# Three of eight top-k masks taken from VectorE and given to ScalarE and GpSimd

## The chip, the cores and the metric

One core of a Trainium2 chip runs the whole program. The metric is device time in microseconds (us) of one execution, median of several runs. TensorE (PE), VectorE (DVE), ScalarE (ACT), GpSimd (POOL) and SyncE (SP, which issues most DMAs) each take their instructions in program order and wait for one another through semaphores.

## The reference

Three stages follow one another: attention in which every query keeps only its 32 largest scores, a routed layer with one expert for each token, and a layer of four experts that are all used.

```python
# attention: batch 2, 8 heads, 576 tokens, head width 64
scores = scale * np.matmul(q, k.transpose(0, 1, 3, 2))
kth = np.partition(scores, -top_k, axis=-1)[..., -top_k:-top_k + 1]     # top_k = 32
scores = np.where(scores >= kth, scores, -1e9)
attn = np.exp(scores - scores.max(-1, keepdims=True))
attn = attn / (attn.sum(-1, keepdims=True) + 1e-9)
x = np.matmul(attn, v)                                    # then 1152 rows of 512
# first layer: 8 experts, 512 -> 1024 -> 512, each token goes to the argmax of its logits
out[mask] = gate_w[mask, None] * (np.maximum(x[mask] @ w1[e], 0) @ w2[e])
# second layer: 4 experts, all of them, weighted by the normalised domain_probs
out += p[:, e:e + 1] * (np.maximum(x @ w1[e], 0) @ w2[e])
```

## The kernel before

The 1152 tokens are nine tiles of 128 rows, in three groups: tiles 0 and 1, tiles 2 to 4, tiles 5 to 8. Attention makes x tile by tile; the two expert layers work on a whole group. While the layers of one group run, attention of the next group's tiles is mixed in; the first group's attention has nothing to be mixed with, and the last group's layers have no attention beside them.

Attention goes by units: a unit is one tile and one pair of heads, `hp` (0 to 3), with `i` = 0 or 1 for the head in the pair. Its steps are laid out by hand: `at_step(n, fn, ...)` puts a call at step `n` of a plan (in half steps), a unit starts every 8 steps (`b0 = SP * j`), and `attention` is a generator that emits one half step at a time. During the expert layers, `pace` advances it in proportion to the TensorE work emitted. So program order on each engine is fixed when the program is built.

For one head the steps are: `sc_mm` (scores, TensorE), `sc_ev` (copy to SBUF, ACT, L465), `top_max` and `top_rep` in turn, four and three times (MAX8 at L477, MATCH_REPLACE8 at L486, DVE), which leave the 32 largest scores in `m`; `p_exp` (exp of the scores, ACT, L494) into a buffer `e0` or `e1` of which there is one each; `p_mask` (L499, DVE), which multiplies `e` by (score >= 32nd score); `p_hi` (half-precision part and row sum, ACT, L514); `p_lo` (the remainder, POOL, L523); `p_tr` (transposing DMA, SP, L528) into `pt`; and `pv_mm` (product with v, TensorE, L553), seven steps after `p_hi`. `finish_tile` (L577) divides by the row sum and gives the rows `xrow`.

In the expert layers every weight block is split in two parts, `whi` (ACT, L1010) and `wlo` = weight - `whi` (L1018, most of them on POOL, some on DVE). TensorE forms `hps` (L1134), ACT and DVE split its ReLU into `hhi` (L1148) and `hlo` (L1151), and TensorE forms `y` (L1107), which ACT or DVE add up in `acc` (L1186, L1188). Transposes `xtp` (L1036) bring rows to the layers. Around the start of a group, small DVE operations choose experts (`gate`, `pick`, `assign`, `compact`; TensorE's `ips` at L916 reads their result `pg` of L906), and POOL fetches rows with gathers (`yg`, L1226).

Of the kernel before, what the change touches and what calls it, by code (L numbers as in the profile page):

```python
# [14 lines left out]
ACTF = mybir.ActivationFunctionType  # L15
ALU = mybir.AluOpType
# [3 lines left out]
TOPK = 32  # L20
# [24 lines left out]
PV0 = 17  # L45
# [4 lines left out]
def kernel(  # L50
# [15 lines left out]
    nc = tc.nc  # L66
    B, H, S, D = q.shape
# [7 lines left out]
    scale = 1.0 / float(D) ** 0.5  # L75
# [27 lines left out]
    with tc.manual_schedule():  # L103
# [116 lines left out]
        def attention(at, start):  # L220
# [58 lines left out]
            units = [(t, hp) for g in GROUPS for t in g for hp in range(H // 2)]  # L279
            NP = len(units)  # L280
            st = {}
# [5 lines left out]
            def at_step(n, fn, *args, half=0):  # L287
                plan.setdefault(round(2 * n) + half, []).append((fn, args))
# [200 lines left out]
            def p_exp(j):  # L489
                z = st[j]  # L490
                z["e"] = []
                for i in range(2):
                    e = w_p.tile([128, S], F32, tag=f"e{i}", name="e")
                    nc.scalar.activation(out=e, in_=z["s", i], func=ACTF.Exp, bias=z["nb"][:, i:i + 1], scale=scale)  # L494
                    z["e"].append(e)

            def p_mask(j, i):
                z = st[j]
                nc.vector.scalar_tensor_tensor(  # L499
                    out=z["e"][i], in0=z["s", i], scalar=z["m"][:, i, TOPK - 1:TOPK], in1=z["e"][i],  # L500
                    op0=ALU.is_ge, op1=ALU.mult)
# [149 lines left out]
            for j in range(NP):  # L651
                b0 = SP * j
                t, hp = units[j]
                lag = PV_LAST[GROUP_OF[t]] if hp == H // 2 - 1 and t in LAST else PV_LAG
                if j:

                    late = t == MIX or (t == MIX + 1 and hp == 0)
                    b2 = -4 if j == 1 else b0 - 9 if late else b0 - 16
                    at_step(b2, q_tr, j)
                    at_step(b2 + 1, q_ev, j)  # L660
                    for i in range(2):
                        at_step(b0 - 5 + 2 * i, sc_mm, j, i)
                        at_step(b0 - 4 + 2 * i, sc_ev, j, i)
                at_step(b0 + 1, top_nb, j)
                at_step(b0 + 5, p_exp, j)
                for i in range(2):
                    b1 = b0 - 1 if (j, i) == (0, 0) else b0
                    for r in range(4):
                        at_step(-18 if (j, r, i) == (0, 0, 0) else b1 + 2 * r, top_max, j, r, i, half=i)
                        if r < 3:  # L670
                            at_step(b1 + 2 * r + 1, top_rep, j, r, i, half=i)
                    at_step(b1 + 7, p_mask, j, i, half=i)
                for i in range(2):
                    at_step(b0 + 8 + i, p_hi, j, i)
                    at_step(b0 + 9 + i, p_lo, j, i)
                    at_step(b0 + 10 + i, p_tr, j, i)
                    at_step(b0 + (lag if j else PV0) + i, pv_mm, j, i)
                if hp == H // 2 - 1:
                    for n in range(3):
                        at_step(b0 + lag - 2 + n, row_factor, t, n)  # L680
                    at_step(b0 + lag + 2, finish_tile, t)
                if hp == 0 and j:
                    at_step(b0 - 28, ld, "q", q, t)
                    b3 = b0 - 16 if t == MIX + 1 else b0 - 21
                    at_step(b3, q_hi, t)
                    at_step(b3 + 1, q_lo, t, nc.gpsimd)
                    at_step(b3 + 3, q_two, t)
# [576 lines left out]
        at = ctx.enter_context(ExitStack())  # L1264
        start = ctx.enter_context(ExitStack())
        att = attention(at, start)
        done = set()

# [214 lines left out]
```

## Time and profile before

| what | us |
|---|---|
| median of 3 runs (918.04 to 923.94) | 921.47 |
| the profiled execution, its own time | 922.85 |
| span of that execution, first to last instruction | 921.1 |
| PE busy in the span | 815.3 |
| DVE busy | 659.2 |
| POOL busy | 534.6 |
| ACT busy | 496.6 |

Rows of the trace speak of the profiled execution, whose time is 1.75 us above its span and 1.38 us above the median. Busy times of PE count pipelined matmuls, so a busy PE is not PE at its peak. Time positions below are microseconds from the start of the span.

### The profile page before, as it was taken

What the parts mean: (1) busy time and instruction counts of PE and PEld (TensorE: products, weight loads), DVE (VectorE), ACT (ScalarE), POOL (GpSimd) and SP (SyncE); (2) the same over time, 40 slices, a digit from 0 to 9 for tenths busy, and PEclk for the clock granted to TensorE, in tenths of its full rate; (3) what the DMA queues carried; (4) which work ended last, traced back from release to release, by engine and by line L of the source; (5) the groups of instructions that cost most, each with busy time, mean ns of one, the idle gap of its engine ahead of it and who ended that gap; (6) DMA issues with size and microseconds to landing.
All of it is one profiled execution on the core that took longest, in us unless ns stands there. A gap on an engine that the chain in (4) does not pass through costs nothing. (4 is left out here: it accounts for less than half of the span.)

```text
span 921.1 us, 15133 instructions
## 1 busy us (share of the span) xinstructions
PE 815.3 (89%) x5277; PEld 696.2 (76%) x5277; DVE 659.2 (72%) x1309; ACT 496.6 (54%) x1017; POOL 534.6 (58%) x469
## 2 busy tenths in 40 slices
PE   5555576999999987999979999998999899999995
PEld 4444365887888876888859888877888688888884
DVE  5999969998989989999989899944434431123212
ACT  6857644765768654677637664633355242432220
POOL 3664456986787975778738676755346343333320
PEclk7675577999999998999989999999999999999998
DMA  7464534867675754679666464554456433322201
GB/s 133 82 128 84 139 104 118 220 177 182 166 184 121 193 157 137 201 180 257 170 122 177 126 172 131 134 148 135 148 163 228 139 115 97 109 91 92 92 23 50
DMA packets 197627, 129.60 MB, mean 141 GB/s; under 512 B 129122, under 2 KB 172130, under 8 KB 197540
## 3 DMA queue, kind: packets, MB, share of 16 engines
q1 hardware_dynamic: 196500, 125.12, 51.2%
q0 software_dynamic: 1040, 3.41, 1.3%
q8 instruction: 43, 0.70, 0.3%
q14 instruction: 44, 0.36, 0.1%
HBM read 98.62 MB, written 6.30 MB: 114 GB/s over the span
## 5 line engine op out<-in xcount | busy, mean ns | idle before, releaser
L1018 POOL TENSOR_TENSOR wlo<-wraw,whi 128x512 fp32r<-128x512 f32 x278 | 364.4, 1332 | 251.1 <-ACT whi L1010 212.6
L1151 DVE SCALAR_TENSOR_TENSOR hlo<-hps,hhi 128x256 fp32r<-128x256 f32 (+3 forms) x168 | 83.7, 498 | 189.0 <-ACT hhi L1148 188.6
L1010 ACT ACTIVATE whi<-wraw 128x512 fp32r<-128x512 f32 x336 | 193.5, 624 | 26.0 <-DMA wraw<-in_moe_w_dram 25.9
L1148 ACT ACTIVATE hhi<-hps 128x256 fp32r<-128x256 f32 (+3 forms) x168 | 75.2, 448 | 230.0 <-PE hps L1134 221.2
L1107 PE MATMUL y<-whi,hhi 128*128 128x512 f32 x440 | 177.6, 404 | 1.0 <-ACT acc L1186 0.6
L1107 PE MATMUL y<-wlo,hhi 128*128 128x512 f32 x440 | 173.4, 394 | 1.1 <-POOL wlo L1018 1.1
L1107 PE MATMUL y<-whi,hlo 128*128 128x512 f32 x440 | 172.9, 393 | 0.6 <-DVE hlo L1151 0.6
L1134 PE MATMUL hps<-x,whi 128*128 128x256 f32 (+2 forms) x768 | 169.3, 344 | 4.2 <-DVE hlo L1151 2.6
L477 DVE MAX8 m<-w 128x8 f32<-128x576 f32 x216 | 154.0, 742 | 0.0
L1134 PEld LDWEIGHTS hps<-x,whi 128*128 128x128 f32 x768 | 131.1, 192 | 19.1 <-DVE hlo L1151 3.7
L523 POOL TENSOR_TENSOR pbuf<-e,pbuf 128x576 f16<-128x576 f32 (+1 forms) x80 | 109.5, 1368 | 48.9 <-ACT pbuf L514 45.3
L486 DVE MATCH_REPLACE8 w<-m,w 128x576 f32<-128x576 f32 x144 | 105.9, 739 | 0.0
L1107 PEld LDWEIGHTS y<-whi,hlo 128*128 128x128 f32 x440 | 83.0, 189 | 19.2 <-DVE hlo L1151 0.9
L1107 PEld LDWEIGHTS y<-whi,hhi 128*128 128x128 f32 x440 | 83.9, 191 | 14.0 <-ACT acc L1186 1.0
L1107 PEld LDWEIGHTS y<-wlo,hhi 128*128 128x128 f32 x440 | 83.8, 190 | 13.3 <-POOL wlo L1018 1.7
L1134 PE MATMUL hps<-x,wlo 128*128 128x256 f32 (+2 forms) x384 | 86.0, 343 | 0.0
L273 PE MATMUL sps<-kst,qs 128*128 128x288 f32 x320 | 64.8, 333 | 19.5 <-ACT s_sb L465 9.5
L499 DVE SCALAR_TENSOR_TENSOR e<-s_sb,m,e 128x576 f32<-128x576 f32 x72 | 78.3, 1115 | 1.1 <-ACT e L494 1.0
L553 PEld LDWEIGHTS <-pt 128*128 128x128 f16 (+3 forms) x1200 | 48.8, 106 | 36.0 <-DMA pt<-pbuf 16.3
L514 ACT ACTIVATE pbuf<-e 128x576 f16<-128x576 f32 (+1 forms) x80 | 54.2, 678 | 38.4 <-DVE e L499 38.0
L553 PE MATMUL pv<-vst,pt 128*128 128x64 f16 (+3 forms) x1200 | 61.8, 203 | 14.8 <-DMA pt<-pbuf 12.8
L273 PEld LDWEIGHTS sps<-kst,qs 128*128 128x128 f32 x320 | 52.9, 212 | 27.7 <-ACT s_sb L465 12.9
(181 smaller groups left out, 1074.2 us busy)
## 6 DMA issues: line engine op xcount, KB each, us to landing
wraw<-in_moe_w_dram SPq DMA_DIRECT2D x168, 512.0 KB, 3.9
x_scr<-xrow SPq DMA_DIRECT2D x9, 256.0 KB, 2.1
out_dram<-acc SPq DMA_DIRECT2D x9, 256.0 KB, 2.3
kraw<-in_k_dram SPq DMA_DIRECT2D x16, 128.0 KB, 3.0
vraw<-in_v_dram SPq DMA_DIRECT2D x8, 256.0 KB, 4.2
qraw<-in_q_dram SPq DMA_DIRECT2D x7, 256.0 KB, 4.6
y_scr<-yr SPq DMA_DIRECT2D x6, 256.0 KB, 4.0
pt<-pbuf SPq DMA_TRANSPOSE x72, 4.6
```

Of the source, the lines that this page charges most:

```text
L273: nc.tensor.matmul(out=ps[:, f, 0:HALF], lhsT=qq[:, n, :], rhs=kst[:, h, b * S + f * HALF:b * S + (f + 1) * HALF], start=(j == 0), stop=(j ...
L477: nc.vector.max(out=z["m"][:, i, 8 * r:8 * r + 8], in_=z["s", i] if r == 0 else z["w"][i])
L486: nc.vector.match_replace(out=z["w"][i], in_to_replace=z["m"][:, i, 8 * r:8 * r + 8], in_values=z["s", i] if r == 0 else z["w"][i], imm_va ...
L499: nc.vector.scalar_tensor_tensor(out=z["e"][i], in0=z["s", i], scalar=z["m"][:, i, TOPK - 1:TOPK], in1=z["e"][i], op0=ALU.is_ge, op1=ALU.mult)
L523: nc.gpsimd.tensor_tensor(out=pb[r, 1, o:o + S], in0=z["e"][i][r], in1=pb[r, 0, o:o + S], op=ALU.subtract)
L553: nc.tensor.matmul(out=po[r, h, :], lhsT=l, rhs=rr, start=(n == 0), stop=(n == len(mms) - 1))
L1010: nc.scalar.activation(out=hi, in_=src, func=ACTF.Copy)
L1018: eng.tensor_tensor(out=lo, in0=src, in1=hi.bitcast(F32), op=ALU.subtract)
L1107: nc.tensor.matmul(out=ys[i][0:rows, :], lhsT=l[:, cs], rhs=r[:, 0, :], start=(f == f0 and m == 0), stop=(f == f1 - 1 and m == 2))
L1134: nc.tensor.matmul(out=hp[:, 0:n], lhsT=l[:, c, :], rhs=r[:, c, x0:x0 + n], start=(m == 0), stop=(m == 3 * KD - 1))
L1148: nc.scalar.activation(out=hhi, in_=hp[:, 0:n], func=ACTF.Relu)
L1151: nc.vector.scalar_tensor_tensor(out=hlo, in0=hp[:, 0:n], scalar=0.0, in1=hhi.bitcast(F32), op0=ALU.max, op1=ALU.subtract)
```

## The change

For every tile but the first, and for the second head (`i` = 1) of the first three pairs, that is heads 1, 3 and 5, the DVE instruction of `p_mask` goes. In its place ACT overwrites the score tile twice: relu(kth - score), then exp(-2^126 times that), which is 1 where the score is kept and 0 elsewhere. POOL then multiplies `e` by it. `p_less` (ACT) stands where the mask stood in the plan, the product half a step to one step later, and for these heads `p_hi`, `p_lo`, `p_tr` and `pv_mm` stand two steps later than before. There are 8 x 3 = 24 such heads of 72.

```diff
+            def by_two(j, i):
+                t, hp = units[j]
+                return i == 1 and t > 0 and hp < H // 2 - 1
+
+            def p_less(j, i):
+                z = st[j]
+                s = z["s", i]
+                nc.scalar.activation(out=s, in_=s, func=ACTF.Relu, scale=-1.0, bias=z["m"][:, i, TOPK - 1:TOPK])
+                nc.scalar.activation(out=s, in_=s, func=ACTF.Exp, scale=-(2.0 ** 126))
+
             def p_mask(j, i):
                 z = st[j]
+                if by_two(j, i):
+                    nc.gpsimd.tensor_tensor(out=z["e"][i], in0=z["e"][i], in1=z["s", i], op=ALU.mult)
+                    return
                 nc.vector.scalar_tensor_tensor(
...
-                    at_step(b1 + 7, p_mask, j, i, half=i)
+                    if by_two(j, i):
+                        at_step(b1 + 7, p_less, j, i, half=i)
+                        at_step(b1 + 8, p_mask, j, i, half=i)
+                    else:
+                        at_step(b1 + 7, p_mask, j, i, half=i)
                 for i in range(2):
-                    at_step(b0 + 8 + i, p_hi, j, i)
-                    at_step(b0 + 9 + i, p_lo, j, i)
-                    at_step(b0 + 10 + i, p_tr, j, i)
-                    at_step(b0 + (lag if j else PV0) + i, pv_mm, j, i)
+                    b4 = b0 + i + (2 if by_two(j, i) else 0)
+                    at_step(b4 + 8, p_hi, j, i)
+                    at_step(b4 + 9, p_lo, j, i)
+                    at_step(b4 + 10, p_tr, j, i)
+                    at_step(b4 + (lag if j else PV0), pv_mm, j, i)
```

## Rows read from the trace of the kernel before

**Rows 1.** The page's slices: busy tenths of PE and DVE in 40 slices.
```profile
PE   5555576999999987999979999998999899999995
DVE  5999969998989989999989899944434431123212
```

**Rows 2.** Windows by stage: busy of each engine (instructions), PEclk, DMA, GB/s.
```profile
core 0: us, PE busy (x) PEld busy (x) DVE busy (x) ACT busy (x) POOL busy (x), PEclk, DMA share, GB/s
55.00:121.00 66.00, 36.97 (x291) 28.93 (x289) 64.82 (x154) 42.72 (x86) 27.45 (x32) 0.60 0.54 121
121.00:160.00 39.00, 27.98 (x178) 24.18 (x179) 31.08 (x67) 21.01 (x46) 25.92 (x23) 0.78 0.43 119
160.00:292.00 132.00, 126.31 (x1010) 110.61 (x1009) 124.34 (x247) 93.35 (x203) 104.95 (x84) 1.00 0.70 176
292.00:336.00 44.00, 40.14 (x387) 34.89 (x386) 42.11 (x82) 29.61 (x61) 42.67 (x34) 1.00 0.69 176
336.00:480.00 144.00, 129.41 (x915) 111.90 (x913) 134.04 (x261) 85.40 (x179) 94.89 (x80) 0.94 0.67 175
480.00:604.00 124.00, 124.00 (x859) 108.63 (x858) 118.89 (x228) 76.84 (x155) 86.57 (x74) 1.00 0.58 153
...
640.00:921.00 281.00, 268.24 (x1288) 224.80 (x1286) 82.19 (x125) 97.67 (x184) 104.46 (x81) 0.99 0.36 115
```

**Rows 3.** The same windows, masks of L499 alone: DVE busy (instructions).
```profile
55.00:121.00 66.00, 8.79 (x11) 0.60 0.54 121
...
160.00:292.00 132.00, 19.04 (x16) 1.00 0.70 176
292.00:336.00 44.00, 4.47 (x4) 1.00 0.69 176
336.00:480.00 144.00, 16.95 (x16) 0.94 0.67 175
```

**Rows 4.** Groups by line and form: busy us, mean ns, idle before and its releaser.
```profile
L523 POOL TENSOR_TENSOR pbuf<-e,pbuf 128x576 f16<-128x576 f32 x64 | 87.9, 1373 | 46.1 <-ACT pbuf L514 43.1 <-PE hps L1134 2.2 <-POOL nb L482 0.7
...
L499 DVE SCALAR_TENSOR_TENSOR e<-s_sb,m,e 128x576 f32<-128x576 f32 x72 | 78.3, 1115 | 1.1 <-ACT e L494 1.0
...
L494 ACT ACTIVATE e<-s_sb,nb 128x576 f32<-128x576 f32 x72 | 51.8, 767 | 1.2 <-POOL pbuf L523 1.2
```

**Rows 5.** Lines L499 and L477: ns min/median/max; who waited for L499.
```profile
L499 DVE SCALAR_TENSOR_TENSOR e<-s_sb,m,e x72: 789/808/1912, 21.6 to 602.0; 128x576 f32<-128x576 f32 x72
...
  ACT pbuf L514: 38.0, 22
...
L477 DVE MAX8 m<-w x216: 700/744/755, 12.4 to 600.2; 128x8 f32<-128x576 f32 x108
```

**Rows 6.** Timeline around 343 us, DVE and POOL: start, us, instruction.
```profile
342.28 1.84 DVE L499 SCALAR_TENSOR_TENSOR e<-s_sb,m,e 128x576 f32<-128x576 f32 x1
...
343.47 1.81 POOL L523 TENSOR_TENSOR pbuf<-e,pbuf 128x576 f16<-128x576 f32 x1
```

**Rows 7.** Timeline of DVE at the end of tile 1: start, us, [idle before].
```profile
120.25 0.67 DVE L577 TENSOR_TENSOR xrow<-pv,rd 128x512 f32<-128x512 f32 x1
...
127.19 0.42 DVE L1151 SCALAR_TENSOR_TENSOR hlo<-hps,hhi 128x256 fp32r<-128x256 f32 x1 [3.74 <-ACT hhi L1148]
```

**Rows 8.** What PE waited for, 160 to 604 us: total, times, longest.
```profile
PE ips L916 <- DVE pg L906: 5.3, 1, 5.3
PE xtp L1036 <- DVE acc L1188: 5.1, 2, 3.5
PE pv L553 <- DMA pt<-pbuf: 4.2, 3, 2.7
...
PE y L1107 <- POOL wlo L1018: 1.1, 1, 1.1
```

**Rows 9.** Timeline of POOL around 320 us: start, us, instruction, count.
```profile
312.46 10.29 POOL L1018 TENSOR_TENSOR wlo<-wraw,whi 128x512 fp32r<-128x512 f32 x7
322.70 2.65 POOL L523 TENSOR_TENSOR pbuf<-e,pbuf 64x576 f16<-64x576 f32 x2
```

**Rows 10.** The chain that ended last, one piece: start, us, what.
```profile
461.68 7.90 DMA yg<-y_scr,pos
```

## The prediction, as it was put on record

> **What bounds the kernel now.** I read the slices first, then the windows by stage, then who waits for whom. The slices [rows 1] show two regimes. DVE is at nine tenths almost without a break to about 600 us and then drops to three or four; PE is at five to seven tenths at the start and at nine from about 160 us on. The windows [rows 2] make stages of it. From 55 to 121 us (attention of tile 1, nothing mixed in) DVE is busy 64.82 of 66.00 us while PE has 36.97 and POOL 27.45: DVE alone is the bound. From 160 to 480 us PE and DVE are both nearly full: PE is idle 132.00 - 126.31 = 5.7 us, then 3.9 us (to 336), then 14.6 us (to 480), DVE 7.7, 1.9 and 10.0 us. From 480 to 604 PE shows no idle time at all although DVE is busy 118.89 of 124, so DVE relief buys nothing there. From 640 us on there is no attention and DVE has 82.19 of 281.00 us. So time can be won only from 55 to 121 us, and from the 24.2 us of PE idle time between 160 and 480 us.
>
> What PE waited for in that middle part [rows 8] says who could give it back: 5.3 us for DVE's routing result `pg`, 5.1 us for DVE's `acc`, 4.2 us for transposed probabilities `pt`, which pass ACT, POOL and SP, and only 1.1 us for POOL's `wlo`.
>
> **What the change removes.** 24 masks. At their mean of 1115 ns [rows 4] that is 26.8 us of DVE, at the median of 808 ns [rows 5] 19.4 us. By stage, from the masks that lie there [rows 3]: three of the eleven from 55 to 121 us (heads 1, 3, 5 of tile 1), 8.79 x 3/11 = 2.4 us; six of sixteen from 160 to 292, 7.1 us; one of four to 336, 1.1 us; six of sixteen to 480, 6.4 us. The rest lies where DVE is not late or PE is full.
>
> **What it adds.** On ACT two instructions for each head. The trace has no in-place Relu or Exp of this size, the nearest row is the exp of the same 128x576 tile, 767 ns [rows 4], so 1.53 us a head, 36.8 us in all. ACT has the room: 93.35 of 132.00 us from 160 to 292, the fullest part. Relu (L1148) and Exp (L494) alternate already, so I price no change of function. On POOL a product of two fp32 tiles for each head; nearest is `p_lo` over the same 576 columns, 1373 ns [rows 4], 33 us in all. POOL has 27.1 us free from 160 to 292 and 49.1 from 336 to 480, but 1.3 us from 292 to 336 [rows 2].
>
> **Waits that it adds.** `p_less` waits on ACT for the last MAX8. Behind it in ACT's queue stand `whi`, `hhi` and `sc_ev`. ACT was held at nearly the same place before: 22 of the `p_hi` waited for a mask, 38.0 us in all [rows 5]. The new wait ends one or two masks earlier and is followed by 1.53 us of work, so ACT comes out at most 0.7 us later than after one 0.81 us mask; I take nothing, covered by ACT's idle time. The product waits on POOL for ACT, with `wlo` and the first head's `p_lo` behind it; PE lost 1.1 us to `wlo` in 444 us [rows 8], so a product's 1.4 us is mostly hidden by blocks prepared ahead. `p_hi` of the second head now waits on ACT for POOL, two steps later than it waited for DVE. `p_lo` of that head comes two steps later while the next unit's exp into the same single `e1` stays where it was: 1.2 us of such waits before [rows 4] may become some ten; what covers them is again ACT's idle time. SP gets the second `pt` two steps later, and PE reads it two steps later, so those transposes keep their lead; the first head's `pt` does not move in the plan, though its `p_lo` now stands behind a product on POOL.
>
> **The sum, stage by stage.** *Tile 1, 55 to 121 us:* DVE runs on to `xrow` at 120.25 [rows 7], which starts the first group; three masks less bring it 2.4 us forward. POOL and ACT have the room, so I take all of it: -2.4 (bounds -3.3 at the mean and 0). *121 to 160 us:* DVE waits 3.74 us before its next `hlo` [rows 7], so the mask that goes there gains nothing; `p_less` of tile 2's head 1 falls among the first `whi` and `hhi` and can push the routing by between 0 and 1.5 us: +0.5. *160 to 292:* 7.1 us off DVE against 5.7 us of PE idle time, which is scattered and in part chained (PE, ACT and DVE in turn for transposes): -1.0 (bounds -5.7 and +2). *292 to 336:* here POOL is the late one. Seven `wlo` run for 10.29 us right up to the two `p_lo` at 322.70 [rows 9], and PE's longest wait for `pt` (2.7 us) follows from it. One product goes into this queue: +1.3 (bounds -1.1 if the mask counts instead, +2.7 if two products do). *336 to 480:* the wait of 5.3 us for `pg` ends a DVE run in which one mask took 1.84 us because POOL worked beside it [rows 6]; that mask goes, -1.8. Smaller waits of `hps` for DVE: -1.0. The other large gap is a gather of 7.90 us [rows 10] that POOL starts and the `acc` of rows 8 wait for; a product before it would delay it by 1.4 us, while the `p_lo` that moves two steps later may leave its place in front of it, so 0. Together -2.8 (bounds -6.4 and +1.4). *480 us on:* 0. Sum: -2.4 + 0.5 - 1.0 + 1.3 - 2.8 = -4.4. The profiled execution took 922.85, so 918.4; it lies 1.38 above the median of 921.47, so a median near 917. With the inner bounds of each term the case spans 913 to 922.
>
> **A rule against it.** The rows show first that DVE and POOL disturb one another: a mask beside a POOL operation took 1.84 us [rows 6], one alone 0.81, while MAX8 never leaves 700 to 755 ns [rows 5]. The Trainium skill, Perfetto Trace Analysis, Optimizing Scalar/DVE Operations, warns that since both share an SBUF read port, "offloading operations between those two might not help". The trace agrees for two-input operations and not for MAX8. By the rows the sum keeps its 2.4 and 2.8; by that rule both would be near 0. It is the second rival below.
>
> **The rivals.** *All DVE lag is PE idle time.* If every microsecond of DVE relief from 160 to 480 us came back as PE time, the terms are -2.4, -5.7 (no more idle there), -1.1 and -6.4: 921.5 - 15.6 = 906. For it: DVE has a queue behind it nearly always [rows 2]. Against: the waits named in rows 8 that a mask can shorten are about half of that idle time. *The relief is eaten by contention.* Each product meets one two-input DVE operation and stretches it by 1.84 - 0.81 = 1.03 us: 24.7 us are back on DVE, only the costs of 0.5 and 1.3 stay: 923. Against: after the last MAX8 of a unit DVE does the other mask at once, then mostly MAX8 and MATCH_REPLACE8, and the product starts 1.5 us after. *POOL becomes the bound, slower.* Place: 160 to 336 us, where POOL is busy 147.6 of 176 us and seven products add 9.6 us. If each pushes `wlo` and the first head's `p_lo`, and so `pt`, past what PE has in hand, it costs 9.6 there, 1.4 at the gather and 1.5 in the routing, against the 2.4 won: 921.5 + 10.1 = 932. It decides from the point where POOL's queue is later than the lead of `pt`, as it already is at 322 us; elsewhere POOL still has pauses.
>
> **How the numbers follow.** A measurement of this kernel tells about 1% from no change. The forecast has 0.50 (917, 913 to 922), full relief 0.20 (906), contention 0.18 (923), POOL-bound 0.12 (932). The range for 8 in 10 runs from 905, which takes in most of the full relief, to 929, short of most of the POOL-bound case. Faster by over 1% (below 912.3) is the full relief and a little of the forecast, 0.22; slower by over 1% (above 930.7) is most of the last, 0.11; within, 0.67.
>
> **What would show it.** In the profile after: `xrow` of tile 1 near 117.9 instead of 120.25; DVE busy some 20 to 27 us less, POOL some 33 more, ACT some 37 more; the wait of `ips` for `pg` near 3.5 us; the wait of `pv` around 330 us longer, not shorter; 480 to 604 us as full as before. The prediction is wrong if PE waits for `wlo` or `pt` by more than some 5 us more (POOL), if the 48 masks that stay have a higher mean than 1115 ns (contention), or if PE's idle time from 160 to 480 falls by ten or more.

## The result, and the profile after

The changed kernel takes 934.1 us (median of 4 runs, 931.38 to 935.99), the kernel before 922.64 beside it (918.04 to 923.94): ratio 1.0103, interval 1.007 to 1.0136 (the two medians alone give 1.0124, so the loss is 9.5 to 11.5 us). The forecast was 917.0 with 905 to 929, so the time came out on the other side and outside the range. The profiled execution of the kernel after took 934.64, its span 932.8.

The page's busy times of the kernel after; those of before are in the table ahead of the prediction:

```profile
PE 825.6 (89%) x5277; PEld 704.8 (76%) x5277; DVE 648.4 (70%) x1285; ACT 526.4 (56%) x1065; POOL 562.9 (60%) x493
```

ACT has 29.8 us more and POOL 28.3 more, somewhat less than the forecast 37 and 33. DVE has 10.8 us less, not 20 to 27, and PE has 10.3 us more with the same 5277 matmuls: its work itself became slower.

To see where the time went I matched the k-th `hps` matmul of one trace with the k-th of the other. The kernel after stands +0.1 us against before at 163 us, +3.4 at 298, +7.6 at 311, +4.5 at 366, +11.7 at 378, and from there 11 to 12 to the end. So the loss lies between 163 and 391 us of before, with its largest steps at 298 to 311 and 366 to 378; a third, 3.1 us in small pieces, lies between 231 and 261 us, and 3.2 us are won back between 331 and 351. From 391 us on nothing more is lost. The stretch from 163 to 485 us of before is 163 to 496.5 us after, with the same 2330 matmuls. Windows of the two kernels (columns as in rows 2), before:

```profile
163.00:485.00 322.00, 297.87 (x2330) 259.38 (x2329) 302.42 (x593) 210.31 (x449) 242.32 (x199) 0.97 0.69 176
```

and after, the whole stretch, then the part of it that is 366 to 391 us in before:

```profile
163.00:496.50 333.50, 305.30 (x2330) 265.01 (x2329) 297.77 (x582) 226.81 (x476) 260.26 (x214) 0.95 0.65 171
...
370.50:402.20 31.70, 27.91 (x156) 23.57 (x156) 26.38 (x44) 17.98 (x36) 19.86 (x17) 0.81 0.57 168
```

PE's idle time went from 24.13 to 28.20 us, 4.1 more; the other 7.4 us are PE busy longer over equally many matmuls, at a mean granted clock of 0.95 instead of 0.97. As an estimate from these clocks, (1 - 0.95) x 333.5 - (1 - 0.97) x 322 = 7.0 us, so the clock accounts for nearly all of it. The short stretch took 25.00 us before, at a clock of 0.92, and has 0.81 now.

The new instructions and their neighbours in the kernel after, by form (mean ns of one | idle before and its releaser):

```profile
L515 DVE SCALAR_TENSOR_TENSOR e<-s_sb,m,e 128x576 f32<-128x576 f32 x48 | 56.5, 1194 | 1.9 <-ACT e L494 1.8
L494 ACT ACTIVATE e<-s_sb,nb 128x576 f32<-128x576 f32 x72 | 52.4, 768 | 14.9 <-POOL pbuf L539 14.9
L513 POOL TENSOR_TENSOR e<-e,s_sb 128x576 f32<-128x576 f32 x24 | 35.7, 1486 | 28.3 <-ACT s_sb L508 28.2
L507 ACT ACTIVATE s_sb<-s_sb,m 128x576 f32<-128x576 f32 x24 | 18.6, 773 | 17.0 <-DVE m L477 16.8
L508 ACT ACTIVATE s_sb<-s_sb 128x576 f32<-128x576 f32 x24 | 16.5, 686 | 0.8
```

The sizes are nearly as priced: 773 + 686 = 1459 ns on ACT for a head (forecast 1.53 us) and 1486 ns on POOL (1373). ACT's wait of `exp` for `p_lo` rose from 1.2 us [rows 4] to 14.9.

Who waited for whom in the matched stretch after (us in total, times, longest); rows 8 answer to the PE rows:

```profile
DVE hlo L1172 <- ACT hhi L1169: 16.5, 15, 2.5
ACT s_sb L507 <- DVE m L477: 15.4, 7, 8.4
ACT e L494 <- POOL pbuf L539: 13.6, 6, 3.2
POOL e L513 <- ACT s_sb L508: 7.5, 5, 3.0
PE ips L937 <- DVE pg L927: 6.2, 1, 6.2
PE pv L569 <- DMA pt<-pbuf: 3.5, 3, 1.8
PE qtp L323 <- ACT qs L331: 2.8, 1, 2.8
PE hps L1155 <- DVE hlo L1172: 2.8, 6, 0.7
PE y L1128 <- DVE wlo L1039: 2.1, 1, 2.1
```

PE waits no longer for `pt` than before (3.5 against 4.2) and not for POOL's `wlo`. What grew stands behind ACT: DVE's `hlo` waits 16.5 us for ACT's `hhi` (before, in its matched stretch, 2.5), and PE waits for `hlo` and for ACT's `qs`. An earlier DVE waits longer of itself, so this wait is read again below, beside the relief alone.

The first large step, timeline of the kernel after (start, us, instruction, [idle before]):

```profile
299.69 2.65 POOL L539 TENSOR_TENSOR pbuf<-e,pbuf 64x576 f16<-64x576 f32 x2
...
302.38 0.78 ACT L494 ACTIVATE e<-s_sb,nb 128x576 f32<-128x576 f32 x1 [1.98 <-POOL pbuf L539]
...
305.02 0.78 ACT L507 ACTIVATE s_sb<-s_sb,m 128x576 f32<-128x576 f32 x1
305.83 0.69 ACT L508 ACTIVATE s_sb<-s_sb 128x576 f32<-128x576 f32 x1
...
309.05 0.60 ACT L331 ACTIVATE qs<-qtp 128x512 fp32r<-128x512 f32 x1
...
309.70 0.66 PE L323 MATMUL qtp<-ident,qrow 128*128 128x128 f32 x4 [2.84 <-ACT qs L331]
310.96 0.63 PE L1128 MATMUL y<-whi,hhi 128*128 128x512 f32 x1
```

`p_lo` of the head two steps later holds `e1`, ACT's exp waits 1.98 us for it, `p_less` adds 1.47 us, `qs` is late and PE waits 2.84 us. PE had been busy 2.86 of the 5.50 us from 304 to 309.5, at the full clock. Then the clock falls: this `y` takes 0.63 us where the same form took 0.40 at 303 us, and in the window from 312 to 314 us the granted clock is 0.50, the lower level of 1.2 GHz, with PE busy 2.00 of 2.00 us.

The second large step:

```profile
370.63 0.78 ACT L507 ACTIVATE s_sb<-s_sb,m 128x576 f32<-128x576 f32 x1 [8.37 <-DVE m L477]
...
372.81 1.19 POOL L948 DMA_INDIRECT xg<-x_scr,ixi  x1 [8.47 <-ACT pbuf L530]
...
373.40 5.27 DVE L1039 TENSOR_TENSOR wlo<-wraw,whi 128x512 fp32r<-128x512 f32 x1 [0.22 <-issue]
...
374.04 1.42 POOL L513 TENSOR_TENSOR e<-e,s_sb 128x576 f32<-128x576 f32 x1
375.41 1.28 POOL L539 TENSOR_TENSOR pbuf<-e,pbuf 128x576 f16<-128x576 f32 x1
376.66 0.23 POOL L482 TENSOR_SCALAR nb<-m 128x2 f32<-128x2 f32 x1
376.86 1.26 POOL L1039 TENSOR_TENSOR wlo<-wraw,whi 128x512 fp32r<-128x512 f32 x1
...
378.72 0.51 PE L1128 MATMUL y<-wlo,hhi 128*128 128x512 f32 x1 [2.13 <-DVE wlo L1039]
```

This is head 3 of tile 5. DVE's `wlo`, an operation on two tiles that takes 0.67 us alone, whose `whi` ACT makes behind `p_less`, lasts 5.27 us: it begins beside the gather, POOL then runs the product, `p_lo`, `nb` and its own `wlo` without a pause until 378.12, and DVE is done 0.55 us after that. In before the same DVE instruction met the gather alone:

```profile
369.32 0.67 DVE L1018 TENSOR_TENSOR wlo<-wraw,whi 128x512 fp32r<-128x512 f32 x1
```

### The profile page after: what moved, and what is told of

It is laid out like the page before. It is cut to its first block, busy times and chain, and to the rows that moved or that the text cites. A ratio compares the mean times of both kernels' runs of the same rounds, so it can differ in the third digit from the quotient of the medians.

```text
span 932.8 us, 15107 instructions
## 1 busy us (share of the span) xinstructions
PE 825.6 (89%) x5277; PEld 704.8 (76%) x5277; DVE 648.4 (70%) x1285; ACT 526.4 (56%) x1065; POOL 562.9 (60%) x493
## 4 chain that ended last, share of the span: by engine, by line
PE 61%; DVE 16%; ACT 7%; DMA 6%; issue 4%; POOL 4%; SPq 1%; POOLq 0%; ACTq 0%; DVEq 0%
PE hps L1155 26%; PE y L1128 25%; DVE m L477 4%; DVE w L486 4%; PE pv L569 3%; DMA pt<-pbuf 3%; PE sps L273 3%; POOL wlo L1039 2%; ACT whi L1031 1%; DMA wraw<-in_moe_w_dram 1%; PE xtp L1057 1%; DVE wlo L1039 1%; ACT pbuf L530 1%; DVE hlo L1172 1%; PE qtp L323 1%
## 5 line engine op out<-in xcount | busy, mean ns | idle before, releaser
L477 DVE MAX8 m<-w 128x8 f32<-128x576 f32 x216 | 154.1, 743 | 0.0
L539 POOL TENSOR_TENSOR pbuf<-e,pbuf 128x576 f16<-128x576 f32 (+1 forms) x80 | 106.6, 1332 | 19.5 <-ACT pbuf L530 16.1
L273 PE MATMUL sps<-kst,qs 128*128 128x288 f32 x320 | 66.9, 342 | 13.0 <-ACT s_sb L465 9.5
L273 PEld LDWEIGHTS sps<-kst,qs 128*128 128x128 f32 x320 | 55.0, 220 | 20.7 <-ACT s_sb L465 13.0
L1155 PEld LDWEIGHTS hps<-x,wlo 128*128 128x128 f32 x384 | 66.4, 193 | 5.4
L1039 DVE TENSOR_TENSOR wlo<-wraw,whi 128x512 fp32r<-128x512 f32 x58 | 53.5, 923 | 18.9 <-ACT whi L1031 16.4
```

Source lines behind the costliest of these rows:

```text
L273: nc.tensor.matmul(out=ps[:, f, 0:HALF], lhsT=qq[:, n, :], rhs=kst[:, h, b * S + f * HALF:b * S + (f + 1) * HALF], start=(j == 0), stop=(j ...
L477: nc.vector.max(out=z["m"][:, i, 8 * r:8 * r + 8], in_=z["s", i] if r == 0 else z["w"][i])
L539: nc.gpsimd.tensor_tensor(out=pb[r, 1, o:o + S], in0=z["e"][i][r], in1=pb[r, 0, o:o + S], op=ALU.subtract)
L1039: eng.tensor_tensor(out=lo, in0=src, in1=hi.bitcast(F32), op=ALU.subtract)
L1155: nc.tensor.matmul(out=hp[:, 0:n], lhsT=l[:, c, :], rhs=r[:, c, x0:x0 + n], start=(m == 0), stop=(m == 3 * KD - 1))
```

## Experiments

Theory: ACT's two instructions and POOL's product each cost PE time although both engines have idle time, since all three engines pass on what PE waits for; the cost outweighs a relief of DVE that is real. Rivals: the moved steps, the single `e1`, the contention of DVE with POOL, or a few unlucky meetings. Ratios are against the kernel before on the same chip; 1% of it is 9.2 us.

**Relief alone.** The 24 masks are left out and nothing stands in their place, so the scores of these heads aren't masked; once with the later steps of the change and once at the old ones.

```diff
-                    if by_two(j, i):
-                        at_step(b1 + 7, p_less, j, i, half=i)
-                        at_step(b1 + 8, p_mask, j, i, half=i)
-                    else:
+                    if not by_two(j, i):
                         at_step(b1 + 7, p_mask, j, i, half=i)
```

> The 24 masks are left out altogether (their probabilities stay unmasked), the later places of p_hi, p_lo, p_tr and pv_mm stay as in the changed kernel. It shows what the relief of VectorE is worth by itself. If the forecast's view of the relief was right and only the cost was wrong: 912 to 917. If VectorE's relief is worth nothing here: 920 to 924. If the later places alone are the loss: 930 or more.

Measured: 913.87 (912.4 to 916.47), ratio 0.9897 (0.9831 to 0.9962).

With the steps at the old places (`b4 = b0 + i`) as well:

> The 24 masks are left out, and p_hi, p_lo, p_tr and pv_mm of these heads stand at their old places. Against the same with the later places (914): if the two steps cost by holding e1 and pt longer, 908 to 911; if they pay by hiding late transposes, 916 to 919; if they don't matter, 912 to 916.

Measured: 915.35, ratio 0.9907 (0.9875 to 0.9938). The two agree within their intervals: the relief is worth 8.6 to 9.5 us, and moving `p_hi` to `pv_mm` two steps costs nothing that can be told. Windows of the late one over the same 2331 matmuls:

```profile
161.80:474.90 313.10, 296.34 (x2331) 259.67 (x2330) 287.20 (x580) 210.63 (x450) 240.74 (x200) 0.98 0.70 181
```

PE's idle time is 16.76 us here against 24.13 before: the relief gives back 7.4 us of it and 1.5 us of PE's busy time.

**ACT's part alone.** Masks left out as above, with the two ACT instructions in place; nothing reads what they write.

```diff
                     if by_two(j, i):
                         at_step(b1 + 7, p_less, j, i, half=i)
-                        at_step(b1 + 8, p_mask, j, i, half=i)
                     else:
```

> As the run with no masks, plus the two ScalarE instructions for each of the 24 heads, which nothing reads (the probabilities stay unmasked). Theory A (ScalarE is late: its own 36 us of work and its wait for the last MAX8 push the weight splits): at least 6 us over the run without masks. Theory P (GpSimd's product makes the loss): within 2 us of it.

Measured: 919.78, ratio 0.996 (0.9931 to 0.999), 0.63% or 5.8 us above the relief alone. To tell ACT's own time from its wait for the last MAX8, the Relu takes its bias from `nb`, which is ready early:

```diff
-  nc.scalar.activation(out=s, in_=s, func=ACTF.Relu, scale=-1.0, bias=z["m"][:, i, TOPK - 1:TOPK])
+  nc.scalar.activation(out=s, in_=s, func=ACTF.Relu, scale=-1.0, bias=z["nb"][:, i:i + 1])
```

> 24 masks left out, the two ACT instructions kept at their place in ACT's queue, but the first takes its bias from the early row maximum's product nb instead of the 32nd score, so that neither waits for the last MAX8; nothing reads what they write. It leaves masking of these heads out. Theory that ACT's cost (the two ACT instructions alone cost some 6 us against the relief alone) comes from waiting for the last MAX8 with other ACT work queued behind: 914 to 915, as without them. Rival that it comes from the 1.45 us of ACT's own time: 919 to 920, as with the wait. In between: both.

Measured: 918.92, ratio 0.9948 (0.9925 to 0.9972), 4.7 us above the relief alone. Forms of this kernel:

```profile
L507 ACT ACTIVATE s_sb<-s_sb,nb 128x576 f32<-128x576 f32 x24 | 18.5, 770 | 0.0
```

There is no wait any more (16.8 us in the kernel after, 16.6 in the run before this one) and nearly the same cost. So it is ACT's own 1.46 us a head that costs; a share of the wait within the intervals, some 3 us, can't be excluded. Its matched windows, and those with the wait:

```profile
162.90:479.20 316.30, 296.66 (x2330) 259.79 (x2329) 286.01 (x580) 226.80 (x476) 240.92 (x200) 0.97 0.69 180
```

```profile
161.40:481.90 320.50, 298.34 (x2330) 260.35 (x2329) 290.38 (x581) 226.61 (x476) 241.11 (x200) 0.97 0.68 177
```

PE is idle 19.64 and 22.16 us, between the relief's 16.76 and 24.13 before, and ACT is busy only 227 of 316 to 321 us. So ACT costs although it is idle for more than a quarter of the time. In the rows with the wait, PE waits 2.1 + 1.7 us for `hlo` (0.6 + 0.3 in the relief alone), and `hlo` waits for `hhi` 12.9 us (9.3, so most of that wait comes with the relief and only some 4 us with ACT's part). Without the wait for MAX8, PE's waits for `hlo` are 0.9 + 0.4 us, hardly more than in the relief, so that path is not what both runs share.

One place shows ACT's own time reaching PE. It is the first large step of above, in the relief alone and then in the run without the wait for MAX8:

```profile
301.29 0.66 PE L323 MATMUL qtp<-ident,qrow 128*128 128x128 f32 x4 [1.31 <-ACT qs L331]
```

```profile
304.88 0.66 PE L323 MATMUL qtp<-ident,qrow 128*128 128x128 f32 x4 [2.69 <-ACT qs L331]
```

In both, ACT's exp had waited for `p_lo` nearly equally long before (1.97 and 1.96 us). The two ACT instructions alone make PE's wait for `qs` 1.4 us longer, about their own 1.46 us. In the run with the wait for MAX8 that exp waits 1.02 us, 0.9 less, and PE's wait for `qs` is 1.65, so the wait for `e1` and the two instructions add up there. In the same run ACT's part also meets the second place, with no product on POOL; its trace loses 3.2 us from 366 to 378 us, of 7.2 in the kernel after and 1.0 in the late relief:

```profile
366.18 3.93 DVE L1038 TENSOR_TENSOR wlo<-wraw,whi 128x512 fp32r<-128x512 f32 x1 [0.21 <-issue]
```

**POOL's part alone.** Masks and `p_less` left out, the product in place, of `e` with itself:

```diff
-  nc.gpsimd.tensor_tensor(out=z["e"][i], in0=z["e"][i], in1=z["s", i], op=ALU.mult)
+  nc.gpsimd.tensor_tensor(out=z["e"][i], in0=z["e"][i], in1=z["e"][i], op=ALU.mult)
```

> As the run with no masks, plus the GpSimd product for each of the 24 heads, of e with itself, so that it waits for no ScalarE mask (the probabilities are squared and unmasked). Theory P (GpSimd's queue: p_lo later, ScalarE's exp held by it, VectorE starved beside it): at least 6 us over the run without masks. Theory A: within 2 us of it. If the loss needs both together, this and the ScalarE run each stay within 4 us and their costs don't add up to the 12 us.

Measured: 922.53 (920.93 to 934.54), ratio 1.0001 (0.9963 to 1.004), 1.04% or 9.6 us above the relief: the product alone eats it all. The profiled execution is a long one of this kernel (929.10), so its waits are read with care; one that neither before nor the relief has in the matched stretch is

```profile
PE xgp L960 <- DMA xg<-x_scr,ixi: 4.3, 1, 4.3
```

PE waits for the third of three gathers that POOL starts there. That the product makes it late is not shown. In the version with eight heads (below) the last product begins 31 us before this gather, and PE waits for it too:

```profile
PE xgp L961 <- DMA xg<-x_scr,ixi: 2.5, 1, 2.5
```

There it landed 7.9 us after its issue (at most 4.8 us in before and 4.6 in the kernel after), so the transfer was long, and why isn't known. PE's other waits in this run that exceed the relief's are spread over `pt` (3.5 against 1.9 us), ACT's `acc` (3.2 against 0.6), DVE's `acc` (3.7 against 2.0) and `hlo` (2.7 against 0.6 before `hps`). The way by which the product costs is thus not shown. Two fills of the score tile on POOL instead of the product, which read nothing (masks and `p_less` are left out again):

```diff
-  nc.gpsimd.tensor_tensor(out=z["e"][i], in0=z["e"][i], in1=z["s", i], op=ALU.mult)
+  for _ in range(2):
+      nc.gpsimd.memset(z["s", i], 0.0)
```

> As the run with the GpSimd product alone, but in place of the product two memsets of the same score tile (the 24 masks are left out). They hold GpSimd's queue for about as long and read nothing from SBUF. If GpSimd's product costs by the time it holds the queue: as the product alone, about 922. If it costs by VectorE's two-input operations that can't read beside it: 914 to 916, as with no product at all.

Measured: 919.53, ratio 0.9941 (0.9911 to 0.9971), 4.1 us above the relief. A form row gives the fill's size:

```profile
L514 POOL MEMSET s_sb<- 128x576 f32 x48 | 27.8, 580 | 3.0 <-ACT e L494 1.6
```

27.8 us in POOL's queue go with 4.1 us, and the same PE wait for the gather stands in its rows with 2.9 us (the gather took 8.4 us), so how much of the 4.1 us is the queue's is open. The product had 31.1 us in the run before this one and cost 9.6; the 12% that it is longer do not make up the 5.5 us between them. That it reads, or that `p_hi` waits for it, may be the rest; which of the two isn't told apart.

**The single `e1`.** The product goes into the score tile, so that `e1` is free two steps earlier.

```diff
-  nc.gpsimd.tensor_tensor(out=z["e"][i], in0=z["e"][i], in1=z["s", i], op=ALU.mult)
+  nc.gpsimd.tensor_tensor(out=z["s", i], in0=z["e"][i], in1=z["s", i], op=ALU.mult)
+  z["e"][i] = z["s", i]
```

> The changed kernel with the product written into the score tile, which p_hi and p_lo then read; so the single buffer e1 is free when the product is done, and the next unit's exp no longer waits for p_lo. If ScalarE's waits for p_lo (13.6 us from 160 to 480 us after the change) make the loss between 290 and 311 us: 927 to 930, and those waits below 3 us. If they are covered: 932 to 936.

Measured: 932.66, ratio 1.0089 (1.0059 to 1.0119). Its form row:

```profile
L494 ACT ACTIVATE e<-s_sb,nb 128x576 f32<-128x576 f32 x72 | 51.6, 767 | 0.0
```

The wait of 14.9 us is gone, and the time is that of the change within the intervals. In its place `sc_ev` waits 3.6 us for `p_lo`, since the score tile is now held longer. At the first large step PE still waits 2.81 us for `qs`, though ACT's exp waits for nothing there (ACT waits 1.61 us for MAX8 instead). Another wait takes its place, so taking away the largest new wait on ACT wins nothing.

**Meetings.** The change without head 3 of tile 5, the one at 372 us (`by_two` ends in `and (t, hp) != (5, 1)`; DVE masks that head):

> The changed kernel, but head 3 of tile 5 keeps its VectorE mask at its old place (23 heads instead of 24). In the trace of the changed kernel its two ScalarE instructions push a weight split by 1.4 us into a run of GpSimd work (gather, product, p_lo, wlo), beside which VectorE's wlo took 5.27 us, and TensorE stood. If that one meeting is what costs there: 926 to 929. If another such meeting takes its place, or the cost is general: 931 to 935.

Measured: 929.11, ratio 1.0059 (1.0019 to 1.0099), 0.44% or 4 us better than the change, with intervals that overlap. The instruction that lasted 5.27 us is short again:

```profile
373.46 0.67 DVE L1039 TENSOR_TENSOR wlo<-wraw,whi 128x512 fp32r<-128x512 f32 x1
```

But this trace falls back by 3.8 us between 378 and 385 us of before, where the third gather landed 8.8 us after its issue and PE waits 3.3 us for it.

Without heads 3 and 5 of tile 4 too, those at the first large step (`(t, hp) not in ((4, 1), (4, 2), (5, 1))`):

> The changed kernel, with DVE's mask kept for three of the 24 heads: 3 and 5 of tile 4 and 3 of tile 5, those that lie at the two places where the trace after falls back (299 to 311 us and 363 to 379 us). Theory of few meetings: the 11.6 us come from these places, so some 922 to 925, no slower than before. Rival, a cost spread over all heads: 21/24 of it stay, 931 to 932. Keeping head 3 of tile 5 alone gave 929.

Measured: 927.81, ratio 1.0055 (1.0034 to 1.0076). It lies between the two theories: three of 24 heads carry about half of the loss, by the medians nearly all of that is one head, and some 5 us are left with 21 heads. The two heads of tile 4 together gain nothing that can be told, although the stall at 309 us is gone (PE waits 0.42 us for `qs`, as in before); the trace falls back at another place instead, by 1.5 us between 163 and 174 us, where a mask was held:

```profile
166.73 3.82 POOL L1039 TENSOR_TENSOR wlo<-wraw,whi 128x512 fp32r<-128x512 f32 x3
...
168.34 4.22 DVE L515 SCALAR_TENSOR_TENSOR e<-s_sb,m,e 128x576 f32<-128x576 f32 x1
...
170.48 1.46 POOL L513 TENSOR_TENSOR e<-e,s_sb 128x576 f32<-128x576 f32 x1
```

**Fewer tiles.** The change for tiles 1, 5 and 6 alone, without head 3 of tile 5 (`t in (1, 5, 6)`, 8 heads):

> The change for tiles 1, 5 and 6 alone, without head 3 of tile 5: 8 heads. GpSimd has room there (31 of 66 and 107 of 144 us busy after the change) and the relief alone won most there. If the cost lies in the stretches where GpSimd is full (160 to 336 us) and in that one meeting: 916 to 920, faster than both kernels. If each product costs wherever it stands: 924 to 928.

Measured: 924.64, ratio 1.0003 (0.9974 to 1.0032), where the second reading had it; the wait of 2.5 us for the gather, shown above, is in its trace. And for tile 1 alone (`t == 1`, 3 heads):

> The change for heads 1, 3, 5 of tile 1 alone. Prediction's term for this stage: -2.4, so 921.5 to 922 where before has 924. What the trace after showed up to 120 us (0.2 to 0.5 us won or lost, since the exp and p_hi on ACT come later): 924, no difference. First hps of the first group and xrow of tile 1 say it more finely than the time.

Measured: 922.93, ratio 1.001 (0.9987 to 1.0032). Neither gains nor loses. No version that keeps all masks beats the kernel before.

## Why the prediction was wrong, step by step

**The step that failed is the pricing of what is added.** "I take nothing, covered by ACT's idle time" and "mostly hidden by blocks prepared ahead" put the two added loads at 0.5 + 1.3 us. Alone, on top of the relief, they measured 4.7 to 5.8 us (ACT) and 9.6 us (POOL). Intervals of single kernels touch; over all executions (13 of the two reliefs, 22 with ACT's part, 10 with POOL's, each divided by the mean of before beside it) the costs are 4.5 us, give or take 1.8, and 9.2, give or take 3.4. Together the change stands 1.0103 - 0.9897 = 2.06%, 19.0 us, above the relief; the parts add up to 15.4. The 3.6 us between lie within the intervals, so that the two make each other worse is not settled by the times; at the meeting at 372 us they may: ACT's part alone already held the DVE instruction for 3.93 us, and with a product in the same POOL run it was 5.27. Idle time of an engine by the window was the wrong measure: ACT works here between PE and DVE (`hhi`, `qs`, `whi`), and an instruction added in its queue delays whichever of these comes next, whatever pause ACT has later; the wait for `qs` at the first large step shows it, 1.31 us without the two instructions and 2.69 with them. For POOL the cost is shown and its way to PE is not.

**The relief was under-priced.** Tile 1, 160 to 292 and 336 to 480 were to win 2.4 + 1.0 + 2.8 = 6.2 us; the relief alone won 8.6 to 9.5. By the matched `hps` of the late version, 1.2 us up to 163 us, 2.3 more to 298, 2.9 to 366 and 3.8 to 485: less than forecast early, more in the middle (at the old steps only 0.9 us come after 391 us, where the late version wins 4.2, so single traces differ). "480 us on: 0" holds for the late version: its advantage is 10.1 us at 485 and at the end. Of the 13.2 us that the full-relief rival priced for the middle, 8.9 came back, 7.4 of them as PE idle time.

**The range.** The bounds written beside the terms add up to -16.5 and +7.6 us, 905 to 929. The narrower 913 to 922 of the forecast follows from no bounds that are written down.

**Tile 1, -2.4.** Without any replacement `xrow` stood 1.3 us earlier, counted from the tile before. With the change it is

```profile
120.75 0.67 DVE L593 TENSOR_TENSOR xrow<-pv,rd 128x512 f32<-128x512 f32 x1
```

against 120.25 [rows 7] and the forecast's 117.9, in a run that was 0.8 us behind at tile 0 already: 0.3 us won, and 0.6 in the kernel with tile 1 alone. ACT's part alone leaves the 1.3 us, POOL's part alone 0.65. Another part of what is lost stands at the mask of head 6:

```profile
109.36 1.55 DVE L515 SCALAR_TENSOR_TENSOR e<-s_sb,m,e 128x576 f32<-128x576 f32 x2 [0.61 <-ACT e L494]
```

DVE runs into ACT's exp there, where before it was the late one. The added work is not the whole reason: the late relief has 0.30 us at this mask, and the relief at the old steps has none. The moved `p_hi` on ACT waits for the transpose of a `pbuf` (2.57 us at 105.67 after, 3.59 in the late relief), and exp stands behind it. So at that place the moved steps, priced at nothing, cost some tenths.

**Waits.** "Some ten" us for `e1` was right in size (14.9). At the first large step the wait did reach PE together with `p_less`, but the kernel that removes it is no faster that can be told. Over the whole kernel the moved steps cost nothing that can be told, as priced. The wait for `pg` did not shrink to 3.5; it is 6.2, and 5.7 (late) or 4.8 (old steps) with the relief alone, so the mask of 1.84 us in rows 6 did not set it. `pv`'s wait around 330 us did not grow.

**The rivals.** *POOL becomes the bound* gave 932, near the result, but not by its mechanism: it had PE wait for `wlo` and `pt` from 160 to 336 us, and PE waits for neither more than before. The one new PE wait in the two runs with POOL's part alone, for the gather `xg` (4.3 and 2.9 us), is there also where no product is near, as shown above, so it isn't shown to be POOL's queue. *Contention* was to put 24.7 us back on DVE. DVE's busy time is 637.1 us with the relief alone, 639.5 with ACT's part, 644.3 with the product and 648.4 with both (635.1 and 638.0 in the other two kernels without masks and product): about 7 to 11 us came back, three to five tenths of that forecast. The sign that I named for it, a mean of the 48 masks above 1115 ns, was badly chosen: it is 1194 after, and 1194 also where no product runs:

```profile
L515 DVE SCALAR_TENSOR_TENSOR e<-s_sb,m,e 128x576 f32<-128x576 f32 x48 | 56.5, 1194 | 1.1 <-ACT e L494 1.0
```

That is the kernel with the relief alone at the old places; the 48 masks that stay are met by POOL's other work. A product on POOL costs 1431 ns at the median (1486 in the mean) for a mask of 808 ns at the median [rows 5], a factor of 1.8. The Trainium skill, GPSIMD Engine Reference, Key points, says that for elementwise work VectorE is about twice as fast; the trace agrees with its 1.8. Moving such an instruction here added more engine time than it took away: 22.1 us of DVE's time (659.2 - 637.1 with the late relief) became 35.1 us on ACT and 35.7 on POOL.

**What stays open.** Some 5 us of the loss are with the 21 heads outside the three and aren't pinned to places, the 3.1 us between 231 and 261 us among them (PE waits 1.80 us for `pt` at 248.31 there, and 0.7 us for `hlo` before). How much of the product's cost is reading and how much `p_hi`'s wait isn't known either, nor what made the third gather long in four of the traces (7.9 and more us in three of them; in the run with POOL's part alone its landing isn't in the trace).

## What to carry to other kernels

When an instruction is moved from a full engine to two that look half idle, price the added time on each of them as if some of it reached the bound: here a sixth of ACT's 35 us and nearly a third of POOL's 31 did, since those engines hand on what the full one and TensorE wait for (seen for ACT at `qs`, argued for POOL). Measure the relief alone first, by leaving the work out: it bounds what the offloading can win, 9 us here, and what replaces the work must cost less than that. And look at what a stall does to the clock, not only at its length.

## What was not expected of the hardware

A two-input instruction of DVE is now and then held through several POOL instructions in a row. In before, a sum of `yg` of this kind lasted 5.07 us:

```profile
461.97 5.07 DVE L1232 SCALAR_TENSOR_TENSOR acc<-yg,gt_all,acc 128x512 f32<-128x512 f32 x1
...
462.72 3.76 POOL L1018 TENSOR_TENSOR wlo<-wraw,whi 128x512 fp32r<-128x512 f32 x3
```

It ended 0.56 us after POOL's last `wlo` (462.72 + 3.76 = 466.48), as the 5.27 us above ended 0.55 us after POOL's run and the 4.22 us 0.62 us after. The Trainium skill, SBUF — State Buffer, Who interferes with whom, says that a VectorE instruction with two SBUF inputs contends with a GpSimd instruction that reads SBUF. The trace agrees, and shows that there are two kinds of hold. The usual one lasts under 2 us and ends with a POOL instruction, even where POOL goes on at once, as here in before beside a `p_lo` that ended at 204.41 us:

```profile
203.51 1.45 DVE L1018 TENSOR_TENSOR wlo<-wraw,whi 128x512 fp32r<-128x512 f32 x1
...
204.38 3.01 POOL L1018 TENSOR_TENSOR wlo<-wraw,whi 128x512 fp32r<-128x512 f32 x2
```

It ended 0.55 us after that `p_lo`, while POOL worked on. Of 137 masks, `wlo` and sums of `yg` on DVE in before, 45 lasted 1 to 2 us, and each of them ended 0.55 to 0.62 us after the end of a POOL instruction; only the sum above lasted longer. The kernel after has three above 2 us, the late relief none. What makes a hold the long kind isn't known, so the long ones can't be priced ahead.

A short stall of PE also cost more than itself. Over the matched stretch of the two profiled executions only 4.1 of 11.5 us are PE idle time; nearly all the rest, by the estimate of 7.0 us above, is matmuls at the lower clock level, 0.63 us for a `y` instead of 0.40, after a wait of 2.84 us that ended at 309.70.
